# First weight blocks one at a time, v of the second pair on GpSimd's queue, and the first down-projection by thirds of w_out

## The chip, the cores and the metric

One core of a Trainium2 chip runs the whole program. The metric is device time in microseconds, from the first instruction to the last of one execution; of several runs the median is taken. TensorE (PE) multiplies matrices and transposes; VectorE (DVE), ScalarE (ACT) and GpSimd (POOL) do elementwise work; SyncE (SP), ACT and POOL issue DMA transfers, which run on 16 DMA engines. Matrix products land in PSUM, 8 banks of 2 KB for each of 128 partitions.

## What is computed

A retention layer (linear attention with a decay per head) and behind it a gated feed-forward layer with an RMS norm:

```python
def _attn_ref(q, k, v):                       # q, k, v: (4, 8, 768, 64) float32
    gamma = 1.0 - 2.0 ** (-5.0 - np.arange(H))
    scale = 1.0 / np.sqrt(D)
    for t in range(S):
        state = gamma * state + np.einsum('bhd,bhe->bhde', k[:, :, t], v[:, :, t])
        y[:, :, t] = scale * np.einsum('bhd,bhde->bhe', q[:, :, t], state)
    return y

def _moe_ref(x, w_gate, w_val, w_out, rms_g): # x: y as (3072, 512); d_ff = 1536
    rms = np.sqrt(np.mean(x * x, axis=-1, keepdims=True) + 1e-06)
    xn = x / rms * rms_g
    g = xn @ w_gate
    silu = g * (1.0 / (1.0 + np.exp(-g)))
    return silu * (xn @ w_val) @ w_out
```

## The kernel before

**Tiling.** The 768 positions of each of the 4 batches are cut into 6 groups `c` of 128 positions. In a group the scores inside it are computed as one masked product; what comes from earlier groups goes through a state matrix. The 4 batches of a group make 512 tokens, which pass the feed-forward layer together. In groups 0 and 1 two batches form a "pair" `p` and share tiles: each has 64 partitions, with two neighbouring positions in a row. From group 2 on each batch has a tile of its own, and q and k are transposed by DMA (`t_dma`) instead of by PE (`tp`).

**The feed-forward layer.** d_ff = 1536 is 12 blocks of 128. `gv(c, n0, n1, t0, t1)` makes blocks n0 to n1 of `xn @ w_gate` and `xn @ w_val` for the tokens t0 to t1, four matmuls of 128x128 weights each, then a Silu on ACT and a product on DVE into `hT`. `down(c, b)` (L548) multiplies the 12 blocks of `hT` of one batch with `wo_b` into one bank, 12 matmuls of 512 columns; ACT copies the bank to `o_sb` (three buffers) and SP stores it. `load_w(n0, n1)` (L83) loads blocks n0 to n1 of both weights, two transfers on POOL's queue that cast float32 to bf16 on the way; `load_wo` (L88) does the same for `w_out`.

**The order** is written out by hand: the source order is the order in which each engine and each queue gets its work, and an instruction waits for its operands in that place. From L568 on the first group is laid out call by call: pair 0's q and k are transposed (`tp`), scores (`ap`), masks (`ap_mask`), values (`y0`), mean square (`squares0`, `eps0`), the power for the norm on POOL (`power`), the normed rows (`norm0`), their transposes (`x_pe`, `x_copy`), and then `gv` for the 256 tokens of that pair; pair 1's steps are woven into these. `v_cast(p)` (L267) makes a bf16 copy of v on ACT, which `y0` reads. `heat(n)` issues n matmuls on constant data, whose result nobody reads, where PE would stand idle. After both pairs, `gv` runs for tokens 256 to 512 and for the remaining blocks, with group 1's first steps in between; then come `y1(0)` (values of group 1, pair 0), `down(0, 0)` to `down(0, 3)`, and group 1's pair 1 between the third and the fourth of them (L680 to L709). From L721 a list of steps (`gv` and `down` of one group) runs with the next group's attention hung in behind given steps.

**Transfers at the start.** POOL issues, in this order: q and k of pair 0, half of its v (the other half is SP's), q and k of pair 1 (L137, L138), and after the iotas and `ya_p` the blocks 0 and 1, then 2 and 3 (L569, L570). The rest follows behind `power(0, 0)`: blocks 4 to 7, `vp_pair(0, 0)`, blocks 8 and 9 (L606 to L609). v of pair 1 is SP's (L587), held back by a dependency until the first mask product is done.

**Banks.** `bank()` gives PSUM banks in a written order (`first`, then `order`); once `split[0]` is set (L723), attention gets banks 0 to 3 in turn and the feed-forward layer 4 to 7.

Of the kernel before, what the change touches and what calls it, by code (L numbers as in the profile page):

```python
# [8 lines left out]
F32 = mybir.dt.float32  # L9
BF16 = mybir.dt.bfloat16  # L10
# [6 lines left out]
def kernel(  # L17
# [11 lines left out]
    nc = tc.nc  # L29
    ctx.enter_context(tc.manual_schedule())  # L30

    B, H, S, D = q.shape
# [32 lines left out]
    def bank(name, dtype=F32, ffn=False, i=None):  # L65
        if i is None and split[0]:
            i = turn[ffn] % 4 + 4 * ffn
            turn[ffn] += 1
        elif i is None and first:
            i = first.pop(0)  # L70
        elif i is None:
            i = order[0]
            order.append(order.pop(0))
        return psum.tile([128, 512 if dtype == F32 else 1024], dtype, name=name, tag=f"p{i}")
# [8 lines left out]
    def load_w(n0, n1, *kinds):  # L83
        sl = slice(n0 * 128, n1 * 128)
        for i in kinds or (0, 1):
            nc.gpsimd.dma_start(out=(wg_b, wv_b)[i][:, :, sl], in_=(wg_v, wv_v)[i][:, :, sl])
# [6 lines left out]
    def load_pair(c, p, n, batches=(0, 1), eng=None, after=None):  # L93
        u = U.setdefault((c, p), {})
        if n not in u:
            if n == "v":
                u[n] = work.tile([128, H, 2 * D], F32, name="v2f", bufs=3)
            else:
                u[n] = work.tile([128, H, 2 * D], BF16, name=n + "2b", bufs=4)
        for b in batches:  # L100
            i = (eng or nc.gpsimd).dma_start(out=u[n][b * 64:b * 64 + 64], in_=pair_v[n][c, 2 * p + b])  # L101
            if after is not None:
                tc.add_manual_dep(i.ins, after.ins.name, SYNC_DEP, reason="transfer order")
# [31 lines left out]
        nc.gpsimd.iota(offp[i * 64:i * 64 + 64], pattern=[[-1, 2], [1, 2], [2, 64]], base=0, channel_multiplier=-2)  # L135
    load_pair(0, 0, "v", (1,))
    load_pair(0, 1, "q")  # L137
    load_pair(0, 1, "k")  # L138
    for i in range(2):
        nc.gpsimd.iota(pos_p[i * 64:i * 64 + 64], pattern=[[C, 2], [1, 2]], base=1, channel_multiplier=2,  # L140
                       allow_small_or_imprecise_dtypes=True)
# [51 lines left out]
    for e in range(2):  # L193
        r = slice(e * 64, e * 64 + 64)
        nc.gpsimd.tensor_tensor(out=ya_p[r], in0=pos_p[r, 1, e:e + 1].to_broadcast([64, H]),
                                in1=lngs[r], op=ALU.mult)

    def exponents():
        nc.vector.tensor_tensor(
            out=va_p, in0=pos_p[:, :, None, :].to_broadcast([128, 2, H, 2]),  # L200
            in1=lngs[:, None, :, None].to_broadcast([128, 2, H, 2]), op=ALU.mult)
        nc.vector.tensor_tensor(
            out=va_n, in0=pos_n[:, :, None].to_broadcast([128, NCH, H]),
            in1=lngs[:, None, :].to_broadcast([128, NCH, H]), op=ALU.mult)
# [11 lines left out]
    def heat(n, i=7):  # L216
        hot = bank("hot", i=i)
        for _ in range(n):
            nc.tensor.matmul(hot, ones[:, :128], ones, start=True, stop=True)  # L219
# [5 lines left out]
    def tp(c, p, n, a, eng=None):  # L225

        u = U[c, p]
        ps = bank("t_ps", BF16)
        view = ps[:, :512].rearrange("p (x b e j) -> p x e b j", x=2, b=2, e=2)
        for x in range(2):  # L230
            for e in range(2):
                for i in range(2):
                    h = 2 * (2 * a + x) + i
                    nc.tensor.transpose(view[i * 64:i * 64 + 64, x, e], u[n][:, h, e * D:e * D + D], ident)  # L234
        u["t_ps", n, a] = ps
        if eng:
            tc_(c, p, n, a, eng)

    def tc_(c, p, n, a, eng):
        u = U[c, p]  # L240
        t = work.tile([128, 2, 2, 2, 64], BF16, name=n + "2T", tag=n + "T", bufs=8)
        copy(eng, t.rearrange("p x b e j -> p (x b e j)"), u["t_ps", n, a][:, :512])
        u[n + "T", a] = t
# [20 lines left out]
            in0=u["a_ps", a][i].rearrange("p (x t) -> p x t", x=2), in1=m, op=ALU.mult)  # L264
        u["am", a, i] = am

    def v_cast(p):  # L267
        u = U[0, p]
        u["vb"] = work.tile([128, H, 2 * D], BF16, name="vb", bufs=2)
        nc.scalar.copy(u["vb"], u["v"])  # L270

    def vp_pair(c, p):
        u = U[c, p]
# [6 lines left out]
    def y0(p, a):  # L280
        u = U[0, p]
        if a == 0:
            u["y"] = [bank("y_ps") for _ in range(2)]
        for x in range(2):
            for i in range(2):
                h = 2 * (2 * a + x) + i
                for e in range(2):
                    for b in range(2):
                        r = slice(b * 64, b * 64 + 64)
                        nc.tensor.matmul(u["y"][b][:, h * D:h * D + D], u["am", a, i][r, x, e, :],  # L290
                                         u["vb"][r, h, e * D:e * D + D],
                                         start=h == 0 and e == 0, stop=h == H - 1 and e == 1, skip_group_check=True)
# [68 lines left out]
    def x_pe(c, p, j):  # L361
        u = U[c, p]
        ps = bank("x_ps", BF16)
        for s in range(KS):
            nc.tensor.transpose(ps[:, s * 128:(s + 1) * 128], u["xn"][j][:, s * 128:(s + 1) * 128], ident)  # L365
        u["x_ps", j] = ps

    def x_copy(c, p, j, eng):
        b = 2 * p + j
        dst = XT[c][:, :, b * C:(b + 1) * C]  # L370
        src = U[c, p]["x_ps", j][:, :512].rearrange("p (s t) -> p s t", s=KS)
        if c == 0 and j == 0:
            nc.vector.tensor_tensor(out=dst, in0=src, in1=g_col[:, :, None].to_broadcast([128, KS, 128]), op=ALU.mult)
        else:
            return copy(eng, dst, src)
# [144 lines left out]
    def gv(c, n0, n1, t0, t1):  # L520

        if c not in HT:
            HT[c] = work.tile([128, NFF, GT], BF16, name="hT", bufs=1)
        w = t1 - t0
        m = (n1 - n0) * w
        ps = []
        for wt, name in ((wg_b, "g_ps"), (wv_b, "v_ps")):
            x = bank(name, ffn=True)
            for n in range(n0, n1):
                o = (n - n0) * w  # L530
                for s in range(KS):
                    nc.tensor.matmul(x[:, o:o + w], wt[:, s, n * 128:(n + 1) * 128], XT[c][:, s, t0:t1],  # L532
                                     start=s == 0, stop=s == KS - 1)
            ps.append(x)
        sg = work.tile([128, 512], BF16, name="sg", bufs=4)
        nc.scalar.activation(sg[:, :m], ps[0][:, :m], AF.Silu)  # L536
        return nc.vector.tensor_tensor(  # L537
            out=HT[c][:, n0:n1, t0:t1], in0=sg[:, :m].rearrange("p (n t) -> p n t", t=w),
            in1=ps[1][:, :m].rearrange("p (n t) -> p n t", t=w), op=ALU.mult)
# [8 lines left out]
    def down(c, b):  # L548
        ps = bank("o_ps", ffn=True)
        for n in range(NFF):  # L550
            nc.tensor.matmul(ps, HT[c][:, n, b * C:(b + 1) * C], wo_b[:, n, :], start=n == 0, stop=n == NFF - 1)  # L551
        o_sb = work.tile([128, DM], F32, name="o_sb", bufs=3)
        nc.scalar.copy(o_sb, ps)  # L553
        store(nc.sync, c, b, slice(0, DM), o_sb)

    def down_last(c, b):
        o_sb = work.tile([128, DM], F32, name="o_sb", bufs=3)
        for i in range(2):
            m = slice(i * 256, i * 256 + 256)
            ps = bank("o_ps", ffn=True)  # L560
            for n in range(NFF):
                nc.tensor.matmul(ps[:, :256], HT[c][:, n, b * C:(b + 1) * C], wo_b[:, n, m],  # L562
                                 start=n == 0, stop=n == NFF - 1)
            copy("av"[i], o_sb[:, m], ps[:, :256])
            store(nc.scalar if i == 0 else nc.sync, c, b, m, o_sb)


    begin(0)  # L568
    load_w(0, 2)  # L569
    load_w(2, 4)  # L570

    mask_exp(0)
    mask_exp(1)
    heat(11)
    tp(0, 0, "q", 0, "v")
    tp(0, 0, "q", 1, "v")
    heat(1)
    tp(0, 0, "k", 0, "v")
    tp(0, 0, "k", 1, "v")
    exponents()  # L580
    heat(2)
    ap(0, 0, 0)
    ap(0, 0, 1)
    for a in range(2):
        for i in range(2):
            ap_mask(0, 0, a, i)
    load_pair(0, 1, "v", eng=nc.sync, after=U[0, 0]["mask", 0, 0])  # L587
    v_cast(0)

    g_ps = bank("g_bc_ps")  # L590
# [12 lines left out]
    power(0, 0)  # L603
    tc_(0, 1, "k", 0, "v")
    tc_(0, 1, "k", 1, "v")
    load_w(4, 6)  # L606
    load_w(6, 8)
    vp_pair(0, 0)
# [13 lines left out]
    gv(0, 0, 1, 0, 256)  # L622
    ap_mask(0, 1, 1, 0)
    gv(0, 1, 2, 0, 256)
    v_cast(1)
    ap_mask(0, 1, 1, 1)
    gv(0, 2, 3, 0, 256)
    gv(0, 3, 4, 0, 256)
    y0(1, 0)
    y0(1, 1)  # L630
    squares0(1)
# [47 lines left out]
    gv(0, 11, 12, 0, GT)  # L679
    load(2, 0)  # L680
    y1(0)
    down(0, 0)
    y1_out(0)
    square(1, 0, 0)
    square(1, 0, 1)
# [3 lines left out]
    load(2, 1)  # L689
    vp_pair(1, 1)  # L690
    load(2, 2)
    down(0, 1)
    down(0, 2)
    t_dma(2, 0)
    for n, e in (("q", "a"), ("k", "v")):
        for a in range(2):
            tp(1, 1, n, a, e)
    x_pe(1, 0, 0)
    x_copy(1, 0, 0, "v")
    x_pe(1, 0, 1)  # L700
    x_copy(1, 0, 1, "v")
    ap(1, 1, 0)
    ap(1, 1, 1)
    for a in range(2):
# [1 line left out]
            ap_mask(1, 1, a, i)  # L706
    load(2, 3)
    t_dma(2, 1)
    down(0, 3)  # L709

    def run(steps, after):
        for i, step in enumerate(steps):
# [7 lines left out]

    steps = [L(gv, 1, n, n + 2, t, t + 256) for t in (0, 256) for n in range(0, NFF, 2)]  # L721
    steps += [L(down, 1, b) for b in range(B)]
    split[0] = True  # L723
    run(steps, {
        0: [L(y1, 1), L(y1_out, 1), L(kvp, 1, 1)],
        1: [L(square, 1, 1, 0), L(square, 1, 1, 1), L(rstd, 1, 1), L(state1, 1)],
# [76 lines left out]
```

## Time and profile before

| | |
|---|---|
| median of 11 runs | 239.84 us (238.46 to 241.78) |
| the profiled execution: its time | 240.16 us |
| its span, first to last instruction | 238.4 us |
| PE busy | 226.7 us (95%) |
| PEld (weight loads) busy | 137.5 us (58%) |
| DVE / ACT / POOL busy | 129.3 / 87.6 / 115.7 us |
| chain that ended last | PE 86%, DMA 6%, DVE 3%, POOL 2% |
| granted TensorE clock | 1.0 in the whole span |
| read from HBM / written | 28.32 MB / 6.29 MB |

PE and PEld are the two halves of TensorE, matmuls and the loads of their weights, which overlap. A row of the timeline or of the chain gives the start in us from the span's start, the length, engine, source line and what was done; "out<-in" are tile names. A row of the DMA view gives packets, bytes and rate of a stretch, or, for one issue, the time from issue to landing. The chain of waits is followed back from the last instruction: at each step to what released it.

### The profile page before, as it was taken

The numbers are of one execution on the slowest core, as the hardware profiler recorded it, in microseconds if no ns is written. First come the engines' busy times: TensorE is split into PE (matmuls) and PEld (weight loads), VectorE is DVE, ScalarE is ACT, GpSimd is POOL, SyncE is SP. The second block draws the span as 40 slices with busy tenths as digits, with TensorE's granted clock in tenths as the row PEclk, the third lists the DMA queues.
The fourth block names the chain that finished last, engine by engine and source line by source line (L and its number), as shares of the span: only waits on it lengthen the run. The fifth ranks groups of instructions, "written<-read, shape, count | busy, mean of one in ns | idle before, by whom it ended". The sixth has DMA issues, their size and how long they took to land.

```text
span 238.4 us, 5411 instructions
## 1 busy us (share of the span) xinstructions
PE 226.7 (95%) x2198; PEld 137.5 (58%) x2223; DVE 129.3 (54%) x222; ACT 87.6 (37%) x176; POOL 115.7 (49%) x150
## 2 busy tenths in 40 slices
PE   7885999999999999999999999999999999999993
PEld 2443785545788865585454684444674544854443
DVE  3774634739576585837866336966245742243300
ACT  2964544233253244225324235323325241333221
POOL 8966599739869941971937903917001000000000
PEclk9999999999999999999999999999999999999999
DMA  8999999999999999599999992994510204100022
GB/s 106 162 178 201 169 170 164 198 204 209 169 131 185 201 154 178 110 177 134 106 117 179 110 202 89 110 196 108 159 51 0 44 3 145 75 3 0 0 88 89
DMA packets 83306, 30.24 MB, mean 127 GB/s; under 512 B 69521, under 2 KB 78993, under 8 KB 83282
## 3 DMA queue, kind: packets, MB, share of 16 engines
q0 software_dynamic: 51328, 16.52, 65.1%
q1 hardware_dynamic: 31280, 13.25, 29.3%
q8 instruction: 17, 0.28, 0.5%
q10 hardware_dynamic: 674, 0.14, 0.3%
q14 instruction: 7, 0.06, 0.1%
HBM read 28.32 MB, written 6.29 MB: 145 GB/s over the span
## 4 chain that ended last, share of the span: by engine, by line
PE 86%; DMA 6%; DVE 3%; POOL 2%; issue 2%; DVEq 0%; POOLq 0%
PE v_ps L532 25%; PE o_ps L551 25%; PE g_ps L532 24%; DMA wv_b<-in_moe_w_val_dram 4%; DMA k2b<-in_k_dram 2%; PE y_ps L505 2%; PE a_ps L460 2%; DVE am L262 1%; PE y_ps L489 1%; PE t_ps L234 1%; PE o_ps L562 1%; PE kv_ps L498 1%; PE a_ps L255 1%; PE x_ps L365 1%; POOL q2b L101 1%
## 5 line engine op out<-in xcount | busy, mean ns | idle before, releaser
L537 DVE TENSOR_TENSOR hT<-sg,v_ps 128x512 bf16<-128x512 bf16 (+1 forms) x76 | 49.9, 657 | 75.0 <-PE v_ps L532 72.6
L532 PE MATMUL v_ps<-xnT,wv_b 128*128 128x256 bf16 (+1 forms) x427 | 74.9, 309 | 2.3 <-DMA wv_b<-in_moe_w_val_dram 1.9
L532 PE MATMUL g_ps<-xnT,wg_b 128*128 128x256 bf16 (+1 forms) x415 | 73.5, 307 | 1.5 <-DMA wg_b<-in_moe_w_gate_dram 1.0
L536 ACT ACTIVATE sg<-g_ps 128x512 bf16<-128x512 f32 (+1 forms) x76 | 43.7, 574 | 83.1 <-PE g_ps L532 78.2
L551 PE MATMUL o_ps<-wo_b,hT 128*128 128x512 bf16 x268 | 60.8, 379 | 0.4
L532 PEld LDWEIGHTS <-wv_b 128*128 128x128 bf16 x428 | 41.6, 98 | 23.4 <-DMA wv_b<-in_moe_w_val_dram 2.8
L532 PEld LDWEIGHTS <-wg_b 128*128 128x128 bf16 x428 | 40.3, 98 | 21.1 <-DMA wg_b<-in_moe_w_gate_dram 1.8
L551 PEld LDWEIGHTS <-hT 128*128 128x128 bf16 x276 | 26.5, 98 | 31.4
L429 POOL TENSOR_SCALAR m<-ms 128x2 f32<-128x2 f32 x10 | 2.2, 219 | 68.7 <-ACT xsq L424 68.7
L553 ACT COPY o_sb<-o_ps 128x512 f32<-128x512 f32 x23 | 13.4, 582 | 43.7 <-PE o_ps L551 43.7
L437 DVE SCALAR_TENSOR_TENSOR xn<-x,rstd,g_bc 128x512 bf16<-128x512 f32 x20 | 21.9, 1121 | 12.8 <-POOL rstd L345 12.8
L469 DVE TENSOR_TENSOR am<-a_ps,causal 128x512 bf16<-128x512 f32 x32 | 20.8, 680 | 0.0
L443 POOL TENSOR_TENSOR vp<-v_f,vd_n 128x512 bf16<-128x512 f32 x16 | 20.1, 1277 | 0.0
L113 POOL DMA_DIRECT2D qb<-in_q_dram x16 | 15.0, 938 | 0.6 <-DMA wo_b<-in_moe_w_out_dram 0.6
L424 ACT ACTIVATE xsq<-x 128x512 bf16<-128x512 f32 x20 | 12.4, 623 | 7.7 <-DVE x L415 7.7
L113 POOL DMA_DIRECT2D kb<-in_k_dram x16 | 14.4, 897 | 1.8 <-DMA wo_b<-in_moe_w_out_dram 1.8
L110 POOL DMA_DIRECT2D v_f<-in_v_dram x16 | 14.7, 918 | 0.0
L415 DVE TENSOR_TENSOR x<-y_ps,yd_n 128x512 f32<-128x512 f32 x16 | 10.8, 684 | 0.6 <-PE y_ps L505 0.6
L219 PE MATMUL hot<-ones 128*128 128x512 bf16 x22 | 8.8, 508 | 1.6 <-DVE ones L146 1.4
L275 POOL TENSOR_TENSOR vp<-v2f,vd_p 128x1024 bf16<-128x1024 f32 x4 | 7.8, 1938 | 0.1
L345 POOL TENSOR_TENSOR rstd<-m,mhalf 128x2 f32<-128x2 f32 x10 | 7.2, 718 | 0.8
L101 POOL DMA_DIRECT2D q2b<-in_q_dram x8 | 5.8, 738 | 0.8 <-POOLq L787 0.8
(92 smaller groups left out, 154.9 us busy)
## 6 DMA issues: line engine op xcount, KB each, us to landing
v_f<-in_v_dram POOLq DMA_DIRECT2D x16, 256.0 KB, 7.0
out_dram<-o_sb SPq DMA_DIRECT2D x15, 256.0 KB, 2.3
out_dram<-o_sb SPq DMA_DIRECT2D x17, 128.0 KB, 4.5
qb<-in_q_dram POOLq DMA_DIRECT2D x16, 128.0 KB, 6.4
kb<-in_k_dram POOLq DMA_DIRECT2D x16, 128.0 KB, 6.7
wg_b<-in_moe_w_gate_dram POOLq DMA_DIRECT2D x6, 256.0 KB, 9.1
wv_b<-in_moe_w_val_dram POOLq DMA_DIRECT2D x6, 256.0 KB, 9.6
wo_b<-in_moe_w_out_dram POOLq DMA_DIRECT2D x3, 512.0 KB, 9.5
```

The costliest lines, as they stand in the source:

```text
L110: nc.gpsimd.dma_start(out=x, in_=unit_v[n][c, b])
L113: nc.gpsimd.dma_start(out=x.rearrange("p (h d) -> p h d", h=H), in_=unit_v[n][c, b])
L415: nc.vector.tensor_tensor(out=x[:, :, :, i, :], in0=u["y"][i].rearrange("p (b a d) -> p b a d", b=2, a=NHP), in1=yd_n[:, c, i][:, None, :, ...
L424: nc.scalar.activation(xsq, u["x"][:, b], AF.Square, scale=1.0 / math.sqrt(DM), accum_out=u["ms_"][:, b:b + 1])
L437: nc.vector.scalar_tensor_tensor(out=u["xn"][b], in0=u["x"][:, b], scalar=u["rstd"][:, b:b + 1], in1=g_bc, op0=ALU.mult, op1=ALU.mult)
L443: nc.gpsimd.tensor_tensor(out=x, in0=U[c, b]["v"], in1=vd_n[:, c, :, None].to_broadcast([128, H, D]), op=ALU.mult)
L469: nc.vector.tensor_tensor(out=x, in0=u["a_ps"][i].rearrange("p (a t) -> p a t", a=NHP), in1=causal[:, None, :].to_broadcast([128, NHP, 128 ...
L532: nc.tensor.matmul(x[:, o:o + w], wt[:, s, n * 128:(n + 1) * 128], XT[c][:, s, t0:t1], start=s == 0, stop=s == KS - 1)
L536: nc.scalar.activation(sg[:, :m], ps[0][:, :m], AF.Silu)
L537: return nc.vector.tensor_tensor(out=HT[c][:, n0:n1, t0:t1], in0=sg[:, :m].rearrange("p (n t) -> p n t", t=w), in1=ps[1][:, :m].rearrange( ...
L551: nc.tensor.matmul(ps, HT[c][:, n, b * C:(b + 1) * C], wo_b[:, n, :], start=n == 0, stop=n == NFF - 1)
L553: nc.scalar.copy(o_sb, ps)
```

## The change

Three things are rearranged; what is computed stays.

1. *Transfers at the start.* k of pair 1 is issued after the iotas and `ya_p`; behind it blocks 0 and 1 one at a time (`load_w(0, 1)`, `load_w(1, 2)`), then blocks 2 and 3 together. v of pair 1 leaves SP's queue and its dependency; POOL issues it behind `power(0, 0)`, ahead of blocks 4 to 7. Its bf16 copy is made in two halves of four heads, later in ACT's order. The `heat` calls and the place of `exponents()` differ a little.
2. *Down-projection of group 0.* In place of `down` for one batch after the other, `down_third` takes a third of `wo_b` (4 blocks) for all 4 batches, whose sums stand in 4 banks at a time. The last third goes batch by batch, with pair 1's transposes, normed rows and scores of group 1 between them. Copies and stores come with the last third.
3. `split[0]` is set before the first third.

```diff
     load_pair(0, 1, "q")
-    load_pair(0, 1, "k")
     for i in range(2):
         nc.gpsimd.iota(pos_p[i * 64:i * 64 + 64], pattern=[[C, 2], [1, 2]], base=1, channel_multiplier=2,
...
                                 in1=lngs[r], op=ALU.mult)
+    load_pair(0, 1, "k")
+    load_w(0, 1)
+    load_w(1, 2)
+    load_w(2, 4)
...
-    def v_cast(p):
+    def v_cast(p, *halves):
         u = U[0, p]
-        u["vb"] = work.tile([128, H, 2 * D], BF16, name="vb", bufs=2)
-        nc.scalar.copy(u["vb"], u["v"])
+        if 1 not in halves:
+            u["vb"] = work.tile([128, H, 2 * D], BF16, name="vb", bufs=2)
+        for a in halves:
+            nc.scalar.copy(u["vb"][:, 4 * a:4 * a + 4], u["v"][:, 4 * a:4 * a + 4])
+        if not halves:
+            nc.scalar.copy(u["vb"], u["v"])
...
+    DP = {}
+
+    def down_third(c, t, *bs):
+
+        for b in bs or range(B):
+            if t == 0:
+                DP[b] = bank("o_ps", ffn=True)
+            for n in range(4 * t, 4 * t + 4):
+                nc.tensor.matmul(DP[b], HT[c][:, n, b * C:(b + 1) * C], wo_b[:, n, :], start=n == 0, stop=n == NFF - 1)
+            if t == 2:
+                o_sb = work.tile([128, DM], F32, name="o_sb", bufs=3)
+                nc.scalar.copy(o_sb, DP[b])
+                store(nc.sync, c, b, slice(0, DM), o_sb)
...
     begin(0)
-    load_w(0, 2)
-    load_w(2, 4)
-
     mask_exp(0)
     mask_exp(1)
-    heat(11)
+    heat(12)
     tp(0, 0, "q", 0, "v")
     tp(0, 0, "q", 1, "v")
-    heat(1)
+    exponents()
+    heat(3)
     tp(0, 0, "k", 0, "v")
     tp(0, 0, "k", 1, "v")
-    exponents()
...
-    load_pair(0, 1, "v", eng=nc.sync, after=U[0, 0]["mask", 0, 0])
     v_cast(0)
...
     tc_(0, 1, "k", 1, "v")
+    load_pair(0, 1, "v")
     load_w(4, 6)
...
-    v_cast(1)
     ap_mask(0, 1, 1, 1)
     gv(0, 2, 3, 0, 256)
+    v_cast(1, 0)
     gv(0, 3, 4, 0, 256)
+    v_cast(1, 1)
...
     y1(0)
-    down(0, 0)
+    split[0] = True
+    down_third(0, 0)
     y1_out(0)
...
-    down(0, 1)
-    down(0, 2)
+    down_third(0, 1)
+    for a in range(2):
+        tp(1, 1, "q", a, "a")
+    down_third(0, 2, 0)
     t_dma(2, 0)
-    for n, e in (("q", "a"), ("k", "v")):
-        for a in range(2):
-            tp(1, 1, n, a, e)
-    x_pe(1, 0, 0)
-    x_copy(1, 0, 0, "v")
-    x_pe(1, 0, 1)
-    x_copy(1, 0, 1, "v")
+    for a in range(2):
+        tp(1, 1, "k", a, "v")
+    down_third(0, 2, 1)
+    for j in range(2):
+        x_pe(1, 0, j)
+        x_copy(1, 0, j, "v")
+    down_third(0, 2, 2)
     ap(1, 1, 0)
     ap(1, 1, 1)
...
     t_dma(2, 1)
-    down(0, 3)
+    down_third(0, 2, 3)
...
     steps += [L(down, 1, b) for b in range(B)]
-    split[0] = True
     run(steps, {
```

## The prediction

> **What bounds the kernel now.** I read the windows first, to see where TensorE is not busy, then the chain of waits, to see what it waits for, then the DMA windows, because the chain ends in a transfer. The windows' columns are the stretch, its length, then busy time and instructions of PE, weight loads, DVE, ACT and POOL, the granted clock, the DMA share and GB/s.
>
> ```profile
> 16.00:18.00 2.00, 1.46 (x14) 0.87 (x14) 1.57 (x4) 1.27 (x3) 2.00 (x4) 1.00 1.28 198
> 18.00:20.00 2.00, 0.84 (x8) 0.58 (x7) 0.46 (x1) 1.07 (x2) 2.00 (x2) 1.00 1.37 208
> 20.00:22.00 2.00, 1.37 (x12) 0.82 (x10) 1.92 (x4) 1.22 (x2) 1.74 (x3) 1.00 1.45 197
> 22.00:24.00 2.00, 1.27 (x12) 1.06 (x12) 0.45 (x2) 0.61 (x3) 0.00 (x0) 1.00 1.45 195
> 24.00:26.00 2.00, 1.93 (x44) 1.32 (x43) 1.40 (x4) 1.25 (x4) 0.00 (x0) 1.00 1.46 197
> ```
>
> From 16 to 24 us PE is idle 3.06 of 8 us, the only such stretch (the whole span has PE busy 226.7 of 238.4 us). The chain of waits, start, length and what, says why:
>
> ```profile
> 15.37 0.73 POOL wg_b L86
> 16.09 9.36 DMA wv_b<-in_moe_w_val_dram
> 25.49 0.61 PE v_ps L532 x4
> ...
> 28.16 0.61 PE x_ps L365 x8
> ```
>
> PE starts the weights' matmuls at 17.60, but the step that decides is `wv_b` of blocks 4 and 5, issued at 16.09 and landed at 25.45. Everything that PE gains before 25.45 it gives back in front of that transfer. From it the path runs through three more half-blocks (1.5 us), `kvp` (0.38) and three `heat` matmuls to the transposes of pair 1 at 28.16; behind them PE has no gap worth naming until 47.
>
> The transfers are a queue that is always full. Packets of 512 B (weights), of 256 B (q and k) and of 4 KB (v by POOL) in the DMA view, each from a stretch of its own (21 to 25, 8.5 to 11.5, 12 to 14 and 33.6 to 35 us):
>
> ```profile
> DMA packets 1581, 0.79 MB, mean 196 GB/s; under 512 B 48, under 2 KB 1581, under 8 KB 1581
> ```
> ```profile
> DMA packets 1652, 0.42 MB, mean 138 GB/s; under 512 B 1644, under 2 KB 1651, under 8 KB 1652
> ```
> ```profile
> DMA packets 542, 0.27 MB, mean 134 GB/s; under 512 B 23, under 2 KB 542, under 8 KB 542
> ```
> ```profile
> DMA packets 102, 0.35 MB, mean 252 GB/s; under 512 B 16, under 2 KB 16, under 8 KB 102
> ```
>
> The reader is to see rates: 1581/4 = 395 packets of 512 B per us, 1652/3 = 551 of 256 B, only 542/2 = 271 of 512 B while the first weights start, and 252 GB/s for v. Every weight, q or k transfer is 512 packets, so a weight of two blocks takes 1.30 us of the queue, a q or k transfer 0.93 (0.75 by the 1365 packets of 47.5 to 49.5 us).
>
> **The front, part by part.** *Weights one block at a time.* Two transfers of 512 B packets become four of 512 packets of 256 B. Removed: 2 x 1.30 = 2.6 us. Added: no such weight transfer is in the trace; the q and k rows have the same packets, 4 x 0.75 = 3.0 to 4 x 0.93 = 3.7, taken 3.5 (30 to 32 us shows 1169 in 2 us, 0.88 each). Net +0.9 (+0.4 to +1.1).
>
> The Trainium skill ("DMA: Bandwidth & Descriptors", Specifications) speaks against this part: it asks for 512 B at least for line rate and has read-modify-write below that. By it a small packet would cost as much as a large one, 4 x 1.30 = 5.2, net +2.6 (an estimate with its rule); the row of 256 B packets, 551 per us against 395, speaks for less.
>
> *v of pair 1 from SP to POOL, behind the first power.* From 15 to 19 us both queues run: 806 packets on POOL's, worth 2.04 us at 395 per us, so the 817 of SP's took the other 1.96; all 1024 of v cost 2.46. On POOL's queue 2 x 256 KB at 252 GB/s take 2.08. Net -0.4. But now v comes after blocks 2 and 3, and nothing competes with the first weights. POOL issues two more, 2 x 0.70 (the v rows of the timeline), between `power` (ends 15.37) and the weights of blocks 4 to 7: these go from 15.33 to 16.8, `vp_pair(0, 0)` from 18.32 to 19.8, blocks 8 and 9 from 20.16 to 21.7. Each still has more than 2 us of queue before it. A POOL issue also waits for the eighth transfer before it: at 43.92 one stood 0.32 us for a `wo_b` issued eight earlier. So block 4 cannot be issued before block 0 has landed, about 16.5 to 17.4; that costs the issue 0 to 0.6 us and the landing nothing. Behind that wait on POOL stand `vp_pair(0, 0)` (read at 26.91 by `kvp`) and `power(0, 1)` (26.48): 4 us of room.
>
> *k of pair 1 behind the iotas and `ya_p`* (0.34 + 0.15 + 0.47): issued 1.0 us later, at 8.26; it landed at 12.45 and is read at 13.38, so 0.1 us at most. The six weight issues take 9.64 to 14.2, just ahead of `power` at 14.65.
>
> *Uneven start.* k's last transfer landed at 12.45, wv of blocks 4 and 5 at 25.45: 13.0 us for 6 x 1.30 + 2.46 = 10.3 us of work. 2.7 us were lost, visible in the 271 packets per us and in the first weight landing 7.9 us after its issue. How much of it goes with smaller first packets and no SP traffic is the largest unknown: nothing, or all 2.7 (the q and k transfers just before lost nothing at 551 per us). I take a third, -0.9, because what slows the first touch of the weights is not shown to depend on the size.
>
> Sum for the deciding transfer: +0.9 - 0.4 - 0.9 = -0.4, landed at 25.1. The other chain into 28.16 has room: blocks 2 and 3 land about 20.3 (22.75 + 0.9 - 2.46 - 0.9), v at 22.4, its cast by halves 2 x 0.55 (1.04 for the whole) hides the second half behind the first eight heads' `y0`, so `y0(1)` ends at 23.7 instead of 24.88 and the norm is 1.2 us early. Front: **-0.4 us** (-2.9 to +0.8).
>
> *heat(12), heat(3), exponents.* The first 11 take 4.87, a twelfth ends at 6.76; the transposes wait until 6.61 now: +0.1, and k's landing at 8.3 covers it. Two more behind the q transposes (0.21 each once warm) sit in the gap from 7.63 to 8.44, the exponents (0.38) in DVE's gap from 7.88 to 8.89. Nothing, while k lands at 8.3; without that 0.8 us.
>
> **The down-projection.** The chain from 48.62 on:
>
> ```profile
> 48.62 7.50 PE o_ps L551 x34
> 56.12 1.01 PE t_ps L234 x32
> 57.14 0.33 PE x_ps L365 x4
> 57.47 0.01 issue
> 57.47 0.40 PE x_ps L365 x4
> 57.87 0.69 PE a_ps L255 x32
> ```
>
> 48.18 to 61.09 is 12.91 us. The work: 48 x 0.216 (36 in 7.77 late in the span) = 10.36, transposes 1.01, eight more 0.45 (the row at 71.48), scores 0.57 (at 42.54): 12.39. So 0.5 us is waiting, for `xn` (DVE, until 57.41) and for copies. In the new order ACT's squares no longer stand behind the first `o_sb` copy (50.98 to 51.46), so `xn` is 1.7 us early, and four matmuls lie between each step and its reader: **-0.5** (0 to -0.5). The banks of PSUM come free in time: the first third takes the banks of `v_ps` of block 10, whose product ends at 46.02, of two `kv_ps` (47.87) and, at 50.7, of the second `y_ps` (49.67). `wo_b`'s thirds landed at 43.7, 46.2 and 48.9, now read at 48.2, 51.6 and 55: no wait, before as after.
>
> *What it moves late.* All four copies and stores fall into 56.3 to 62, and SP's queue is in order: store 0, the transposes of batch 0, stores 1 and 2, the transposes of batch 1, store 3. The last `kT` of pair 0 was issued at 62.22 and took 9.7, landed 71.9, read at 73.61: 1.7 us of room. Two stores (4 x 0.55) and the wait for copy 2 put it at 64.4 to 65.0, PE comes 0.8 earlier, at 72.8. With 9.7 it lands at 74.1 to 74.7, 1.3 to 1.9 late; with the 7.4 that is the median of these transposes, never late. Loads of group 2 now come 1.7 us earlier, which should shorten it: I take **+0.4**. The fourth `o_sb` copy also waits for store 0 (three buffers), about 0.7 us in front of ACT's next Silu, whose product is not read for 3 us.
>
> **Sum.** -0.4 - 0.5 + 0.4 = -0.5 us. The profiled execution (240.16 us, span 238.4, 1.76 around it) would become 239.7; it lies 0.3 above the median of the 11 runs, which becomes **239.4**. This case by itself: 238.7 to 240.4. Chance 0.42.
>
> **Rivals.** *The uneven start goes altogether.* For it: q and k at 551 per us directly before. Against it: the slow rate begins with the first touch of the weights, and that remains. The deciding weight lands at 23.3, the norm chain (y0 ends 21.9, + 3.28 as now from 24.88 to 28.16) binds at 25.2: -2.9 - 0.5 + 0.4 gives 236.8; half of it 238.2. Chance 0.33.
>
> *Small packets cost like large ones.* 5.2 instead of 3.5 us, the weight lands at 26.8: +1.3 - 0.5 + 0.4 gives 241.0. For it: nothing in the trace, a cast of f32 weight rows in 512 B pieces is not in it. Chance 0.13.
>
> *The transposes behind the stores.* One place, the scores of group 2 at 73.6, that wait for `kT` of batch 1. At 9.7 us or more from issue to landing PE stands 1.3 to 2.2 us; from 1.3 us on it eats both gains. 239.84 - 0.9 + 2.2 = 241.1. For it: SP in order and 9.7 at this spot; against: 7.4 in the median. Chance 0.12.
>
> **How the numbers follow.** 0.5% is 1.2 us, about what a measurement can tell from no change: below 238.6, above 241.0. Faster: 0.33 and a little of the likeliest, 0.36. Slower: 241.0 and 241.1 lie on the bound, so some two thirds of these, with a rest for what I don't see, 0.19. Same: 0.45. The range leaves out the far end of the first rival (236.8) and holds the others: 237.6 to 241.2.
>
> **What would show it.** Right: `v_ps` of block 0 directly behind its `g_ps` at 17.9, no 1.16 us wait, yet PE waiting at blocks 4 and 5 for a weight that lands near 25; scores of pair 1 with no gap before them near 59.5. Wrong: that weight before 24 or after 26.5; PE waiting at the scores of group 2; or a wait at 8.4 that is longer than now.

## The result, and the profile after

| | before | after |
|---|---|---|
| median | 239.54 us (50 runs) | 243.25 us (13 runs, 240.6 to 244.87) |
| ratio | | **1.0104 [1.0076, 1.0133]** |
| the profiled execution: time / span | 240.16 / 238.4 us | 244.87 / 242.8 us |
| time outside the span | 1.76 us | 2.07 us |
| PE busy | 226.7 us | 228.2 us |

The kernel is slower, by more than the measurement's uncertainty, and the predicted 239.4 us with its range of 237.6 to 241.2 missed it. The ratio is formed from nine of 15 executions (the 13 above and two more, of 241.35 and 250.59 us) and leaves out the six of 244.25 us and more, so it lies below the quotient of the two medians, 1.0155. The profiled execution is at the upper end of the runs, so its loss of 4.71 us is more than the usual one.

The windows of the changed kernel over the stretch in which PE had been idle, with the same columns as before (length, then busy time and instructions of PE, weight loads, DVE, ACT and POOL, the granted clock, the DMA share, GB/s):

```profile
16.00:18.00 2.00, 1.57 (x15) 1.07 (x16) 1.58 (x4) 1.27 (x3) 2.00 (x4) 1.00 1.25 157
18.00:20.00 2.00, 1.83 (x17) 1.39 (x15) 1.35 (x3) 1.53 (x4) 2.00 (x4) 1.00 1.28 260
20.00:22.00 2.00, 1.48 (x12) 1.18 (x13) 1.53 (x4) 0.25 (x1) 2.00 (x2) 1.00 1.29 185
22.00:24.00 2.00, 0.20 (x14) 0.20 (x15) 0.00 (x0) 0.87 (x3) 1.20 (x2) 1.00 1.49 199
24.00:26.00 2.00, 1.62 (x37) 0.98 (x30) 1.30 (x3) 1.41 (x5) 0.00 (x0) 0.79 1.44 192
26.00:28.00 2.00, 2.00 (x11) 1.35 (x10) 0.81 (x3) 0.58 (x3) 1.42 (x3) 0.50 1.45 196
```

The reader is to see two things. The holes of 16 to 22 us are smaller: PE is busy 4.88 of those 6 us where it was 3.67. But they have come together in one hole, 22 to 24, in which PE is busy 0.20 us, and directly behind it the granted clock, 1.0 in the whole span before, falls to one half. The chain of waits names the hole and shows what the clock does to the steps behind it:

```profile
15.42 0.69 POOL v2f L101
16.10 7.00 DMA v2f<-in_v_dram
...
23.13 0.62 ACT vb L275
23.75 0.28 ACT sg L543
24.03 0.52 ACT vb L275
...
24.59 0.41 PE y_ps L297 x16
25.00 0.78 PE g_ps L539 x4
25.78 0.95 PE v_ps L539 x4
26.73 0.85 PE g_ps L539 x4
27.58 0.85 PE v_ps L539 x4
...
29.69 0.61 PE x_ps L372 x8
```

The chain no longer goes through `wv_b` of blocks 4 and 5 but through v of pair 1: it lands at 23.11, the two halves of `vb` and a Silu between them end at 24.55, and PE, which stood from 21.92 to 23.80 and again for 0.38, makes the second half of `y0`. A half-block (four matmuls), 0.44 us before, then takes 0.78 to 0.95. The transposes of pair 1 begin at 29.69 instead of 28.16.

The first weights go in small packets now; the DMA view of 12 to 14 us, where 542 packets of 512 B had moved:

```profile
DMA packets 979, 0.26 MB, mean 130 GB/s; under 512 B 978, under 2 KB 978, under 8 KB 978
```

That is 490 packets of 256 B per us, near the 551 of q and k: the bytes move no faster (134 GB/s before), but the first block needs half of them and is there earlier (`wg_b` of block 0 lands at 15.0, before at 17.5).

Further on, the waits of PE (us in total, times, longest) and the place of the second one in the chain:

```profile
PE y_ps L297 <- ACT vb L275: 2.3, 2, 1.9
PE a_ps L467 <- DMA kT<-kb: 1.5, 1, 1.5
PE g_ps L539 <- DMA xnT<-xn: 0.8, 1, 0.8
```
```profile
68.86 8.06 DMA kT<-kb
76.97 0.40 PE a_ps L467 x8
77.37 0.98 PE g_ps L539 x8
```

The scores of group 2 wait 1.5 us for `kT` of batch 1, which was issued at 68.86 (62.22 before).

So that the kernels can be compared, each profiled execution is cut at two places: the first `x_ps` of pair 1, and the first `g_ps` behind the scores of group 2 (28.16 and 74.23 before, 29.69 and 77.37 after). The third stretch ends with the last `o_ps` (234.44, 238.73).

| profiled execution | start to `x_ps` | to `g_ps` after the scores | to the last `o_ps` |
|---|---|---|---|
| before | 28.16 | 46.07 | 160.21 |
| after | 29.69 | 47.68 | 161.36 |

The 4.71 us are 1.53 in the front, 1.61 around the scores of group 2, 1.15 later (0.8 of it the wait for `xnT` at 108.7), 0.11 in the tail and 0.31 outside the span.

### The profile page after: what moved, and what is told of

Its sections match the earlier page's. It is cut to its first block, busy times and chain, and to the rows that moved or that the text cites. A ratio compares the mean times of both kernels' runs of the same rounds, so it can differ in the third digit from the quotient of the medians.

```text
span 242.8 us, 5415 instructions
## 1 busy us (share of the span) xinstructions
PE 228.2 (94%) x2200; PEld 138.4 (57%) x2226; DVE 127.9 (53%) x222; ACT 87.6 (36%) x177; POOL 118.5 (49%) x154
## 4 chain that ended last, share of the span: by engine, by line
PE 75%; DMA 10%; DVE 7%; POOL 2%; ACT 2%; issue 2%; SPq 0%; DVEq 0%; ACTq 0%; POOLq 0%
PE v_ps L539 23%; PE g_ps L539 22%; PE o_ps L558 17%; PE o_ps L571 4%; DMA kT<-kb 3%; DMA v2f<-in_v_dram 3%; DMA k2b<-in_k_dram 2%; DMA xnT<-xn 2%; PE y_ps L512 2%; PE a_ps L467 1%; DVE am L265 1%; DVE hT L544 1%; PE t_ps L237 1%; PE o_ps L583 1%; DVE xn L444 1%
## 5 line engine op out<-in xcount | busy, mean ns | idle before, releaser
L539 PE MATMUL v_ps<-xnT,wv_b 128*128 128x256 bf16 (+1 forms) x427 | 75.8, 312 | 0.9 <-DMA wv_b<-in_moe_w_val_dram 0.6
L558 PEld LDWEIGHTS <-hT 128*128 128x128 bf16 x228 | 22.0, 98 | 26.1
L444 DVE SCALAR_TENSOR_TENSOR xn<-x,rstd,g_bc 128x512 bf16<-128x512 f32 x20 | 20.2, 1039 | 10.5 <-POOL rstd L352 10.5
L560 ACT COPY o_sb<-o_ps 128x512 f32<-128x512 f32 x19 | 11.0, 581 | 33.0 <-PE o_ps L558 33.0
```

Source lines behind the costliest of these rows:

```text
L444: nc.vector.scalar_tensor_tensor(out=u["xn"][b], in0=u["x"][:, b], scalar=u["rstd"][:, b:b + 1], in1=g_bc, op0=ALU.mult, op1=ALU.mult)
```

## The experiments

**The theories.** G, the clock gate: PE's idle time in front of v's cast lowers the granted clock, and that is the loss of the front. S, the transposes: the stores of the thirds stand ahead of `t_dma(2, 1)` on SP, and the scores of group 2 wait. The expectations below also name V (v comes late, and that is the loss, whatever the clock does) and W or P (the small weight transfers are late). Beside them stands my likeliest case of before, in which the deciding transfer sets the front and small packets or the place of v cost or gain a few tenths.

### Each half of the change by itself

`e1_front_only` keeps the new front and takes the old down-projection; `e2_down_only` does the reverse.

```diff
# e1_front_only, against the changed kernel
-    split[0] = True
-    down_third(0, 0)
+    down(0, 0)
...
# e2_down_only, against the changed kernel
-    load_w(0, 1)
-    load_w(1, 2)
-    load_w(2, 4)
+    load_w(0, 2)
+    load_w(2, 4)
...
+    load_pair(0, 1, "v", eng=nc.sync, after=U[0, 0]["mask", 0, 0])
-    load_pair(0, 1, "v")
...
-    v_cast(1, 0)
-    v_cast(1, 1)
+    v_cast(1)
```

> The new transfers and front with the old down-projection. Theory G (PE stands idle before the values of pair 1, and the clock gate then halves TensorE for 3.4 us): the transposes of pair 1's rows start near 29.7 us where the clock falls to 0.5 and near 28.2 where it does not; nothing waits at the scores of group 2 (73.6 in the kernel before, plus the shift); time 239.5 to 241.3 us, spread like the changed kernel's. Theory S (all of the loss is SP's queue in the down-projection): same as before, 239.5 us, every execution. Theory W (the smaller weight transfers themselves are late): 29.7 us at clock 1.0.

> The old front with the down-projection by thirds. Theory S: the front ends at 28.2 us as before, the clock stays 1.0, the scores of group 2 wait 1 to 2 us for kT of batch 1, a later wait for xnT of up to 1 us; time 240.5 to 242 us. Theory G alone: no loss, 239.5 us, or 0.1 better.

The front by itself took 242.36 us, ratio **1.0122 [1.0091, 1.0153]**; by the medians that is 2.7 us of the whole change's 3.7. The mean granted clock was 0.992 or 0.993 in each of its six executions: one fall of 3.41 us to one half takes 0.007 off the mean of 240 us. Of the whole change's 15 executions nine have a mean clock under 0.996, with a median span of 242.2 us; that of the other six is 239.2. The thirds by themselves took 240.4 us, 1.0024 [0.9991, 1.0057], which is not clear of no change, with a wide scatter (238.99 to 249.34). The chain of the front by itself:

```profile
15.98 6.82 DMA v2f<-in_v_dram
...
25.86 0.85 PE v_ps L539 x4
26.71 0.85 PE g_ps L539 x4
...
29.32 0.61 PE x_ps L372 x8
```

Same hole, same half clock. In the profile of the thirds by themselves the other wait is there without the new front:

```profile
PE a_ps L460 <- DMA kT<-kb: 1.7, 1, 1.7
```

Its clock fell to one half directly behind that wait, from 76.66 to 80.07. So both waits are there, each with its own half of the change; what S costs in time these two runs do not show.

### Work for PE in the hole

If the clock falls because PE idles, matmuls that nobody reads, put into the hole, must give the time back although they add work. `e3_warm` puts nine into the changed kernel; `g1_warm_gap` puts six into the front by itself, `h2_doubles_warm` six into `f2_doubles` (below), `h1_after_warm6` six into the whole change. Constant data, result unread:

```diff
# e3_warm has heat(9, 2) in this place
+    heat(6, 2)
     y0(1, 0)
     y0(1, 1)
     squares0(1)
```

> The changed kernel with nine matmuls on constants before the values of pair 1, 1.9 us of them, where PE stood idle 1.9 us. Theory G: granted clock 1.0 in every execution, the transposes of pair 1's rows at 28.0 to 28.4 us instead of 29.7, time 1 to 1.5 us below the changed kernel (240.5 to 241.3), and the wait at the scores of group 2 stays. Theory W: rows at 29.7 as before, no gain, or a loss of up to 0.3 us if the nine end after v's cast.

> The new front with the old down-projection and six matmuls on constants (1.3 us) in front of the values of pair 1, where PE stood idle 1.7 to 1.9 us. Theory G (the idle makes the clock gate halve TensorE for 3.4 us, and that is the loss): granted clock 1.0 at 20 to 30 us, rows of pair 1 at 27.8 to 29.2 us, about 5 us behind the landing of v, span 237.8 to 239.2, time 240 to 241.3 and so 1.2 to 2 us below the new front without them (242.4). Theory V (v is late, clock or no clock): span stays at 240, time at 242 or more.

The nine gained nothing: 243.07 us, 1.0156 [1.0115, 1.0198], and two of the six executions had a mean clock under 0.996 all the same. The clock stayed at 1.0 in the profiled execution, but there v landed at 24.38 and `wv_b` of blocks 4 and 5 only at 26.83, so `x_ps` began at 29.55 all the same, and the wait for `kT` was in it too. The six in the front by itself are the clearer test, with one half of the change alone: **240.87 us, 1.0035 [1.0012, 1.0059]**, 1.5 us less than without them (2.1 us by the two ratios, each against runs of the kernel before beside it), with a mean clock of 0.996 or more in all 12 executions. The chain of that kernel:

```profile
17.55 7.96 DMA wv_b<-in_moe_w_val_dram
...
26.17 0.44 PE g_ps L539 x4
26.60 0.44 PE v_ps L539 x4
...
28.23 0.61 PE x_ps L372 x8
```

Half-blocks take 0.44 again, and the path is the one that the prediction named: `wv_b` of blocks 4 and 5, landed at 25.51, then 2.7 us to `x_ps`.

The windows show how little work PE had. Length 3.41 us, each ending where the clock fell, in the changed kernel and in the front by itself; the clock column is still 1.00:

```profile
21.75:25.16 3.41, 1.15 (x36) 0.88 (x35) 0.53 (x2) 1.55 (x4) 1.45 (x2) 1.00 1.49 193
```
```profile
20.90:24.31 3.41, 1.33 (x27) 0.97 (x26) 0.94 (x3) 1.41 (x3) 2.19 (x3) 1.00 1.39 193
```

And the 3.41 us at half clock behind it, of the front by itself:

```profile
24.31:27.72 3.41, 3.41 (x30) 2.52 (x30) 1.69 (x5) 1.19 (x4) 1.25 (x2) 0.50 1.46 196
```

PE had been busy 1.15 and 1.33 of the 3.41 us, and 1.46 in `f2_doubles`. In `g1_warm_gap`, with the six matmuls, no stretch of that length between 13 and 33 us has PE busy for less than 2.39; in the kernel before the least is 1.62. A shallow stretch does not always bring the fall: `e4_t_first` and `h2_doubles_warm` (both below) have one from 22.90 to 26.31 with PE busy 1.16 and 1.36, and their profiled executions kept the clock at 1.0.

The Trainium skill ("TensorE: Matmul & The Clock Gate", Part 1: The HAM clock gate) describes a free-running activity window of 3413 ns after which an idle array gets half its clock. The length agrees with the 3.41 us here. Its rule there to avoid idle gaps of more than some 3.4 us does not cover this case: the longest gap here was 1.9 us.

### What of the front makes the hole

Against `e1_front_only`: v back on SP's queue, behind the first mask (f1); one transfer for blocks 0 and 1 (f2); v on POOL ahead of blocks 2 and 3 (f3); both of the last two (g2).

```diff
# f1_v_on_sp
+    load_pair(0, 1, "v", eng=nc.sync, after=U[0, 0]["mask", 0, 0])
-    load_pair(0, 1, "v")
# f2_doubles
-    load_w(0, 1)
-    load_w(1, 2)
+    load_w(0, 2)
# f3_v_first
-    load_w(2, 4)
+    load_pair(0, 1, "v")
...
-    load_pair(0, 1, "v")
+    load_w(2, 4)
```

> The new front with the old down-projection, and v of pair 1 back on SP's queue behind the first mask; blocks 0 and 1 stay single. Theory V (v of pair 1, put behind blocks 0 to 3, is late, and everything behind its cast with it): v lands near 21 us, no wait for the cast, the transposes of pair 1's rows at 28.0 to 28.4 us, span of the kernel before (237.9 us in the median) or up to 0.5 us less. Theory P (single blocks make the weights late): v early, but wv of blocks 4 and 5 lands at 26 or later and the rows start at 28.7 to 29.2, span about 239. The 0.35 us that the new front adds outside the span: gone if it comes with POOL's transfers of v, still there if with the single blocks or the rest.

> The new front with the old down-projection, blocks 0 and 1 in one transfer each as before, v of pair 1 on POOL's queue behind the first power. Theory V: v lands at 23 us or later as with single blocks, PE waits 1.5 us or more for its cast, the loss of 1.2% stays (242 to 242.6 us). Theory P: the loss goes, 239.7 us.

> The new front with the old down-projection, single blocks 0 and 1, then v of pair 1 on POOL's queue, and blocks 2 and 3 behind the first power. Theory V: v lands near 18.5 us, its cast waits for nothing, rows of pair 1 at 28.0 to 28.5 us; blocks 2 and 3 land near 21.5 and cost PE about what they cost before; span 237.5 to 238.2. Theory P: rows at 29 us or later because wv of blocks 4 and 5 lands after 26.

> The new front with the old down-projection, blocks 0 and 1 in one transfer each, then v of pair 1 on POOL's queue, and blocks 2 and 3 behind the first power. If the 0.35 us outside the span come with the single blocks and the wait comes with v behind blocks 2 and 3, both are gone: v lands near 18.5 to 19 us, rows of pair 1 at 27.4 to 28.2, span 237.3 to 238, outside 1.8, time 239.1 to 239.8, not above the kernel before. If blocks 2 and 3, now issued at 15.4, are late: PE waits over 2 us for them and the clock falls, time 241 or more.

| | time, ratio | v of pair 1 landed | executions with a mean clock under 0.996 | outside the span |
|---|---|---|---|---|
| e1_front_only | 242.36, 1.0122 [1.0091, 1.0153] | 22.80 | 6 of 6 | 2.15 |
| f1_v_on_sp | 240.47, 1.0019 [0.9994, 1.0044] | 20.61 | 5 of 12 | 1.92 |
| f2_doubles | 241.4, 1.005 [1.0019, 1.0082] | 22.75 | 8 of 12 | 1.80 |
| f3_v_first | 240.08, 1.0035 [1.0008, 1.0063] | 19.68 | 5 of 12 | 2.12 |
| g2_double_v_first | 240.42, 1.0043 [1.0012, 1.0075] | 20.9 | 5 of 12 | 1.78 |

The landing of v is that of the one profiled execution. Where v lands near 22.8, 14 of 18 executions lose clock; where it lands by 20.9, 15 of 36, little more than of the kernel before (30 of 87, v at 21.1). In f2 the spans of those that lost it have a median of 239.9, of the others 237.85: 2.05 us. In f1 it is 240.2 against 238.2. That the same kernel loses clock in some executions and not in others would fit windows that run on their own, so that it matters where in them the hole lies; the runs do not show the windows. `e1_front_only` lost clock each time. Moving v alone takes most of the loss away (f1, f3), although the first packets stay small; the larger packets by themselves (f2) take 1 us off the median, 0.35 of it outside the span.

> The new front with the old down-projection, blocks 0 and 1 in one transfer each, v of pair 1 on POOL's queue behind the first power, and six matmuls on constants in front of the values of pair 1. Without them it took 241.4 at a clock below 1 in 8 of 12 executions; at clock 1.0 its span was 237.5 to 238.7. Theory G: clock 1.0, span 237.5 to 238.5 in all, outside the span 1.8, time 239.3 to 240.2, the kernel before or 0.2% better. Theory V: 241 or more as without them.

`h2_doubles_warm` took 239.8 us, **1.0014 [0.9992, 1.0036]**, 1.6 us less than `f2_doubles` (0.9 by the ratios, whose intervals overlap), and only one of its 12 executions had a mean clock under 0.996. It is the best form of the new front, and still no gain over the kernel before.

### The transposes behind the stores

`e4_t_first` issues `t_dma(2, 1)` directly behind `t_dma(2, 0)`; `g3_down_t_first` does so with the old front.

```diff
     down_third(0, 2, 0)
     t_dma(2, 0)
+    t_dma(2, 1)
...
     load(2, 3)
-    t_dma(2, 1)
     down_third(0, 2, 3)
```

> The changed kernel with the DMA transposes of batch 1 issued directly behind those of batch 0, ahead of the stores of batches 1 and 2. Theory S: kT of batch 1 is issued about 2.5 us earlier and lands before PE reads it, no wait at the scores of group 2, time 1.5 to 2.3 us below the changed kernel (240 to 241). Rival: the transposes are slow because of the traffic, not of their place; then the wait stays at 1 us or more and the time is unchanged within 0.5 us.

> The old front with the down-projection by thirds, and the DMA transposes of batch 1 directly behind those of batch 0, ahead of the stores of batches 1 and 2. Theory S (these transposes wait behind the stores): no wait for kT at the scores of group 2, time 239.4 to 239.8, the down-projection gaining 0.1 us or less. Rival: the transposes are slow because of the traffic beside them; then waits of 1 us and more stay in some executions, time 240.4 or more.

> The whole change with six matmuls on constants in front of the values of pair 1. Theory G+S (the front loses through the clock gate, the down-projection through kT behind the stores): the front as in the new front with the same six (rows of pair 1 near 28.2 to 29.2, clock 1.0 until 30 us), the wait for kT of batch 1 at the scores of group 2 stays in a good part of the executions; time between 240.9 (that front with the old down-projection) and 242.5. Theory G alone: 240.9, no more. If the six don't help here: 243.

In both profiles the wait for `kT` is gone: the stretch from `x_ps` to the `g_ps` behind the scores is 46.04 and 45.99 us, where the changed kernel has 47.68 and the kernel before 46.07. But the runs are much slower, not faster: `e4_t_first` 248.27 us at the median (241.6 to 251.14), `g3_down_t_first` 245.19 (239.83 to 250.34), 1.0202 [1.0148, 1.0257] from two executions. The profiled executions, 241.6 and 239.83, are the best of their kind, and what the others spend their time on was not seen. Those have mean clocks of 0.972 to 0.993, so the clock fell in them, by the 0.007 above up to four times; what made PE idle there is not known. As a test of S the two profiles show that the place of the transposes makes the wait; as a remedy the edit failed, against both expectations.

`h1_after_warm6` has the clock at 1.0 in five of six executions, and took 242.93 us, 1.0134 [1.0097, 1.0171], where the same front with the old down-projection (`g1_warm_gap`) took 240.87. Between these two, with the clock held, the thirds cost some 2 us, and the profiled executions show where 1.3 of them are (47.05 against 45.77 in the table below). Other comparisons give less: the six executions of the whole change without a lower clock have a median span of 239.2 us, 0.45 above that of `g1_warm_gap`, and `e2_down_only` is 0.7 above the kernel before by the medians. And against the whole change itself (243.25) the six matmuls took off only 0.3. The issues of SP, start and length, in `h1_after_warm6`:

```profile
57.87 1.17 SPq L551 DMA_DIRECT2D out_dram<-o_sb  x2
59.16 1.36 SPq L458 DMA_TRANSPOSE qT<-qb  x1
60.57 1.32 SPq L458 DMA_TRANSPOSE kT<-kb  x1
61.93 2.95 SPq L551 DMA_DIRECT2D out_dram<-o_sb  x4
65.06 1.95 SPq L458 DMA_TRANSPOSE qT<-qb  x1
67.12 1.48 SPq L458 DMA_TRANSPOSE kT<-kb  x1
```

and in `g1_warm_gap`:

```profile
58.05 1.35 SPq L458 DMA_TRANSPOSE qT<-qb  x1
59.51 1.26 SPq L458 DMA_TRANSPOSE kT<-kb  x1
60.94 1.25 SPq L458 DMA_TRANSPOSE qT<-qb  x1
62.30 2.23 SPq L458 DMA_TRANSPOSE kT<-kb  x1
```

The last `kT` is issued 4.8 us later: 1.1 because the first transpose stands behind store 0, 3.0 for stores 1 and 2, 0.7 because the second q transpose's issue is longer (1.95 against 1.25). It takes 8.08 us to land, and PE waits:

```profile
PE a_ps L467 <- DMA kT<-kb: 0.9, 1, 0.9
```

The stretches of the runs that bear on it:

| profiled execution | start to `x_ps` | to `g_ps` after the scores | to the last `o_ps` |
|---|---|---|---|
| e1_front_only | 29.32 | 46.07 | 160.22 |
| e4_t_first | 29.18 | 46.04 | 160.22 |
| f2_doubles | 29.28 | 46.07 | 160.21 |
| f3_v_first | 27.45 | 45.80 | 160.21 |
| g1_warm_gap | 28.23 | 45.77 | 160.21 |
| h1_after_warm6 | 28.59 | 47.05 | 160.21 |
| e2_down_only | 28.47 | 47.91 | 161.88 |
| e3_warm | 29.55 | 46.63 | 160.21 |

The thirds show up in the second column, and only with a late `kT`: 46.63 to 47.91 with the wait, 46.04 without it, against 45.77 to 46.07 for the old order. In the third column `e2_down_only` has its half clock (76.66 to 80.07), as the whole change has the wait for `xnT`; the other kernels with thirds lose nothing there.

The first column does not tell G from V in single executions. With the clock at 1.0, `x_ps` began at 29.18 in `e4_t_first` (v landed at 24.21), at 29.05 in `h2_doubles_warm` (`wv_b` at 26.33) and at 29.55 in `e3_warm`, as late as with the fall, because a transfer came later there. What speaks for G is that added matmuls, which load nothing, brought the front by itself from 242.36 to 240.87 us and its clock to 1.0.

## Why the prediction was wrong, point by point

**The front** was forecast at -0.4 us and cost +1.5 in the profiled execution. *Right:* the single blocks landed early, `v_ps` of block 0 stood directly behind its `g_ps` (17.92), and the packets of 256 B did not cost like large ones: at 490 per us a transfer of 512 takes 1.04 us, between the 0.88 that I took and the 1.30 of large ones. *Wrong by little:* the deciding `wv_b` landed at 25.64 (25.51 in `g1_warm_gap`), where 25.1 was forecast and 25.45 stood before, so the sum of -0.4 for it came out as +0.2, and the runs do not separate its terms; v landed at 23.11 instead of 22.4, and the second half of the cast was not hidden, since a Silu of 0.28 us stands between the halves and ends at 24.03; `y0(1)` ended at 25.0, not 23.7. With the clock at 1.0 that is hardly a loss: 25.64 + 2.7 = 28.3, against 28.16. But the room of the other chain was used up: from the end of `y0(1)` to `x_ps` the norm takes 3.05 us in `f3_v_first`, and 25.0 + 3.05 = 28.05.

**The step that failed** is the sentence "the norm is 1.2 us early": it treats idle time of PE in front of v's cast as free because another chain ends later. It was not free. The change filled the gaps of 16 to 22 us, so that the waiting for v became one hole, and behind it the clock fell to one half for 3.41 us, in which the path to `x_ps` lies. No term of the sum, and no rival, had the granted clock in it, although the windows that I showed have it as a column. The size: 29.69 - 28.3 = 1.4 us in the profiled execution; with the old down-projection 1.5 in the runs (242.36 to 240.87), 1.6 in the other pair (241.4 to 239.8). In the whole change the same six matmuls gave back only 0.3 (243.25 to 242.93), so for it the share of the clock is argued from its halves and its trace, and not shown by a run.

**Heat, exponents, k of pair 1** were forecast at nothing, and the first k transposes are at 8.50 where they were at 8.44: right.

**The down-projection** was forecast at -0.5 us and gave -0.06 (49.70 to 62.55 is 12.85, before 12.91); in `e4_t_first` the whole second stretch, 46.04 us, is within 0.03 of the old order. The waiting was there, and most of it went: the eight `x_ps` took 0.73 in the old order and 0.45 in the new, the scores 0.69 and 0.57, as the sum had it. The mis-sized term is the 12.39 us of work, which came to 12.85 (two gaps of 0.15 us in it lie where one matmul of a group of four has no row). Five lines of the chain after the change:

```profile
58.25 0.64 PE t_ps L237 x16
58.89 0.97 PE o_ps L571 x4
59.86 0.45 PE x_ps L372 x8
60.30 0.86 PE o_ps L571 x4
61.17 0.57 PE a_ps L258 x32
```

I had priced each kind of matmul from a stretch of its own kind. The group of four `o_ps` behind the transposes of k took 0.97, not 4 x 0.216 = 0.86 (the one behind `x_ps` did take 0.86), and sixteen transposes by themselves took 0.64, where half of 32 would be 0.51. Cutting the down-projection into groups made more such changes of kind, and they cost what the removed waits had given.

**The late transposes** were taken at +0.4 us, with a rival of 1.3 to 2.2. The mechanism was right and the place too; the size was nearer to the rival: a wait of 1.5 us, with the issue at 68.86 where I had 64.4 to 65.0. I left out that store 0 also holds back the transposes of batch 0 (60.27 against 57.98), and took an issue of a transpose at its earlier length (the q one of batch 1 took 2.25 us instead of 1.30). I gave this rival 0.12, because its condition was a landing time of 9.7; it came true with 8.06, as the issue was so late.

**Outside the span** there was no term either. The time holds some 2 us more than the span, and by the medians of the runs it is 1.78 to 1.81 us with the first two blocks in one transfer, 2.11 to 2.16 with single blocks and v on POOL, 1.92 with single blocks and v on SP. That 0.34 us is 0.14% of the time and more than a third of what `g1_warm_gap` still loses.

**What stays open:** why most executions with the transposes of both batches in front are 3 to 10 us slower; what the 0.34 us outside the span are spent on; why the thirds cost 0.5 to 0.7 us in two comparisons and 2 in the third; and why work in the hole, which gave 1.5 us back to the front by itself, gave next to nothing to the whole change. By the medians of all executions the halves do add up: 2.7 us for the front and 0.7 for the thirds, against 3.7 for both.

## What to carry to other kernels

Idle time of TensorE off the critical path is not free where it gathers: add up PE's busy time over each 3.41 us in front of a path of matmuls, and where it is under half, as in the front here, expect that the clock can fall in a part of the executions and price it at some 1.5 to 2 us, or fill the hole with a few matmuls (six of 512 columns kept the mean clock at 0.996 or more in 12 of 12 executions of one front and 11 of 12 of another). Price mixed work on PE from a mixed stretch, not from pure ones: each change of kind cost up to a tenth of a microsecond here. When a store is put ahead of a transpose on an in-order queue, follow the whole queue to the last transfer that something waits for.

## What the runs showed of the hardware that was not expected

- In the profiled executions the clock falls for one stretch of 3.41 us, mostly after 3.41 us in which PE was busy 1.13 to 1.67 (1.13 in `g2_double_v_first`, 1.61 in `f1_v_on_sp`, 1.67 in `e2_down_only`). The least busy such stretch of the kernel before has 1.62, and some of its executions have a lower mean clock as well (30 of 87 under 0.996, median span 238.7 against 237.7 for the rest). Two falls, in `g2_double_v_first` at 12.88 and in `g3_down_t_first` at 12.87, came after stretches with PE busy 2.45 and 2.75 of 3.41 us, with scores, values and two matmuls of a one-row weight (`g_bc_ps`, 1.12 us in `g2_double_v_first`) in them, so busy time alone does not tell.
- Transposes by DMA, issued earlier, removed a wait and made most executions slower by far (245.19 and 248.27 us at the median).
- Time outside the span is not constant for a program of the same inputs: 1.78 us with one transfer for the first two weight blocks, 2.12 with two and v on POOL, 1.92 with two and v on SP.
